# A shifted copy of v in an attention and gMLP kernel: engine copies or SBUF-to-SBUF transfers

## The chip, the core and the metric

The kernel runs on one core of a Trainium2 chip. The core has a matrix engine (TensorE, PE in the profile; its weight loads are PEld), a vector engine (VectorE, DVE), a scalar engine (ScalarE, ACT), a general engine (GpSimd, POOL) and a queue engine (SyncE, SP), which here issues nearly all DMA transfers. SBUF is the on-chip memory of 128 partitions, PSUM the accumulator memory of TensorE, used as 8 banks of 128 x 512 float32. Times are device microseconds of an execution; lower is better.

## The reference

Eight batches of eight heads, 576 positions and 64 features go through causal attention with a window of 64, then, with the heads side by side as 512 features, through a gMLP block (a gated layer that mixes positions with a 576 x 576 matrix).

```
scores = scale * q @ k.T                    # per batch and head, 576 x 576
mask   = (rel >= 0) & (rel < 64)            # rel = query position - key position
attn   = softmax(where(mask, scores, -1e9))
x      = attn @ v                           # heads laid side by side: 576 x 512
h      = relu(x @ w_in);  u, w = halves of h (512 columns each)
w_n    = (w - mean) / sqrt(var + 1e-6)      # over the 512 columns
w_s    = w_spatial @ w_n + b_spatial        # mixes the 576 positions
out    = (u * w_s) @ w_out
```

## The kernel before, in words

Every piece of work is a step with a name, a fixed piece of code and a set of engines that could do it (`Plan.add`, line 176). A text, `ORDER` (line 18), lists all 1117 steps in the order in which they are emitted. Each word is `name:engine:buffers`. `as_listed` (line 185) reads it and the loop at line 924 emits the steps. Every engine carries out its own steps strictly in that order, and semaphores hold a step until what it reads is there and the buffer that it writes is free. SP does the same with its list of transfers: an issue that has to wait holds up every later issue. `DQ` issues a transfer on SP as soon as its turn comes; `DG` does so behind the last matmul emitted ahead of it (`behind`, line 297), so the transfer is held back until TensorE has come that far.

The steps of a batch b, with the letters that the order uses, are these.

- ldq, ldk, ldv: loads of q and k (two halves of four heads each) and of v (five pieces of 128 positions, the last of 64). The v loads move runs of 64 float32, 256 bytes.
- cq, ck: casts of q and k to float16 (buffers nq, nk to hq, hk); tq, tk: transposes on VectorE into qT and kT.
- cv: the casts of v into `hv` (two steps of two pieces each). `hv` holds v in float16 as partition = position within 128, piece, head, feature.
- sl, su, s4: the copy of v shifted by 64 positions, `hs`. sl copies partitions 0 to 63 of pieces 1 to 3 of hv to the same place in hs, su copies partitions 64 to 127 of each piece of hv to the same partitions of the next piece of hs, and s4 casts the last 64 positions straight from the load. So piece c of hs holds positions 128c to 128c+63 in its lower half and the 64 positions ahead of them in its upper half; no row changes its partition.
- S: the scores of four heads in blocks of 64 keys, in four PSUM banks; E: the exponentials on ScalarE; M: the mask, a minimum on VectorE; Z: row sums by a matmul with ones; N and n: logarithm and exponential that turn a row sum into its inverse; P: attention times v; X: the product with the inverse, into x. A suffix r is the last 64 positions of all heads.
- P reads keys in blocks of 128 positions that start at multiples of 64. Even starts come from hv and odd starts from hs, which is why the shifted copy is needed: `vv = hv.t if c % 2 == 1 or c == 0 else hs.t` (line 592 on).
- V and U: the two halves of x @ w_in, Vr and Ur their ReLU on ScalarE; Vb and Va the mean and variance on VectorE (tiles st and mv); L1 and L2 the inverse root; A the normalization (tile vn); G: w_spatial times vn; Ge: the gate (tile g); O: times w_out; Oe: evacuation on ScalarE; st: the store.

Batch 0 gets hv in another way (`run_steps`, line 484): v is loaded in long runs (ldx), cast (cx), and put in order by matmuls with a selection matrix (pick, Y), and evacuated (F). Its shifted copies are engine copies too (sl0_0x, su0_0x and so on). Weights are loaded (ldwin, ldwsp, ldwo), cast (cwin, cwsp, cwo), and w_spatial is transposed on TensorE (W) and evacuated (We, tile wspT).

The work of the batches overlaps: while TensorE does V, U, G and O of one batch, the attention of the next is under way. A copy helper, `cp` (line 301), picks the engine's form of copy; on POOL it cuts a cast of q or k into three instructions and one of v into one for each piece. `cost` (line 314) lists the engines that a copy may go to. The buffers are few: two each of hv, hs and of the v load, eight of the other loads (`BUFS`, line 152).

The copies of v for batches 1 to 7 are made in `value_steps` (line 441). In the order before, they stand on these engines: batch 1 on POOL (sl1_0) and VectorE (three), batch 2 on POOL and ScalarE (sl2_1), batch 4 on POOL and ScalarE (sl4_0), batch 6 on POOL and ScalarE (sl6_1, su6_1), and batches 3, 5 and 7 on POOL alone.

Of the kernel before, what the change touches and what calls it, by code (L numbers as in the profile page):

```python
# [18 lines left out]
D0:PE:0 D1:PE:1 ldk0_0a:DQ:0 ldx0_0:DQ:0 D2:PE:2 ldk0_0b:DQ D3:PE:3 D4:PE:4 ldq0_0a:DQ:1 ldq0_0b:DQ  # L19
ldk0_1a:DQ:2 cq0_0a:POOL:0 D5:PE:5 pick:DVE:0 D6:PE:6 ck0_0a:ACT:1 D7:PE:7 D8:PE:0 tk0_0a:DVE:0  # L20
ldq0_1a:DQ:3 D9:PE:0 D10:PE:0 D11:PE:0 ck0_0b:ACT cx0_0:DVE:2 D12:PE:0 D13:PE:0 ldq0_1b:DQ D14:PE:0
ldk0_1b:DQ Y0_0:PE:0:1:2:3 cq0_0b:POOL F0_00:ACT:0 ldx0_1:DQ D15:PE:4 ck0_1a:POOL:3 tk0_0b:DVE
F0_01:ACT ldwsp0:DQ:4 D16:PE:4 D17:PE:4 ldwsp2:DQ:5 tq0_0a:DVE:1 F0_02:DVE D18:PE:4 tq0_0b:DVE
ldwsp1:DQ:6 ldwin10:DQ:7 ldv0_4:DQ D19:PE:4 F0_03:ACT D20:PE:4 cq0_1a:DVE:1 sl0_0x:ACT:0
tk0_1a:DVE:2 D21:PE:4 cq0_1b:POOL tq0_1a:DVE:3 D22:PE:4 cwsp0:POOL ck0_1b:DVE ldwin11:DQ:0
tq0_1b:DVE D23:PE:4 S0_0:PE:4:5:6:7 E0_02:ACT:0 tk0_1b:DVE E0_03:ACT E0_00:ACT:1 S0_1:PE:0:1:3:2
E0_01:ACT su0_0x:DVE M0_00:DVE cwin110:POOL ldq1_0:DG:1 cx0_1:ACT:2 E0_10:ACT:2 Y0_1:PE:6:7:4:5
ldk1_0:DG:3 M0_01:DVE E0_12:ACT:3 F0_12:DVE E0_11:ACT F0_10:DVE S0_r:PE:0:4:3:6 cwsp4:DVE D24:PE:1
ldb:DQ:2 E0_13:ACT E0_r0:ACT:0 M0_10:DVE cwin111:POOL Z0_01:PE:1 D25:PE:2 cwsp1:DVE M0_11:DVE
ldwin01:DQ:5 Z0_00:PE:2 E0_r1:ACT E0_r2:ACT cwsp3:DVE F0_11:ACT cq1_0:POOL:0 cwsp2:DVE E0_r3:ACT  # L30
Z0_10:PE:0 N0_01:ACT:0 N0_10:ACT:1 Z0_11:PE:4 F0_13:ACT ldwin00:DQ:4 N0_00:ACT:2 M0_r:DVE P0_01:PE:3
W4:PE:7 W3:PE:6 sl0_1x:DVE n0_01:ACT su0_1x:DVE n0_00:ACT P0_00:PE:1 N0_11:ACT:3 P0_11:PE:0
n0_10:ACT cwin010:POOL cwin101:DVE Z0_r:PE:5 P0_10:PE:2 We3:DVE n0_11:ACT s40_:DVE X0_00:DVE:1
P0_r:PE:6 W2:PE:4 N0_r:ACT:4 W1:PE:1 cwin100:ACT W0:PE:5 ldk1_1:DG:6 X0_01:DVE X0_10:DVE:2
ldq1_1:DQ:0 We4:DVE V0a_3:PE:3 We0:ACT X0_11:DVE V0a_2:PE:2 V0a_0:PE:7 ck1_0:ACT:1 We2:DVE
tq1_0:DVE:4 V0b_2:PE ldwo0:DQ:7 tk1_0:DVE:5 We1:ACT V0b_3:PE n0_r:ACT V0a_1:PE:5 V0b_0:PE ldwo1:DQ:1
ldv1_0:DG:1 Vr0_2:ACT:0 X0_r:DVE:0 Vr0_0:ACT:1 ldv1_1:DG cwin011:POOL V0b_1:PE S1_0:PE:0:4:1:2
ldv1_2:DQ Vr0_3:ACT:2 cwin000:POOL Vr0_1:ACT:3 ldv1_3:DG Vb0_2:DVE:0 V0_4:PE:6 E1_00:ACT:0
Vr0_4:ACT:4 Vb0_0:DVE:1 Vb0_3:DVE:2 cwin001:POOL Va0_2:DVE E1_02:ACT:1 E1_03:ACT Vb0_1:DVE:3
U0_4:PE:7 Va0_3:DVE E1_01:ACT ldv1_4:DG ck1_1:POOL:3 Vb0_4:DVE:4 Va0_0:DVE Va0_1:DVE Va0_4:DVE  # L40
cb:POOL tk1_1:DVE:0 U0_3:PE:3 L10:ACT:0 ldk2_0:DG:3 L20:ACT cq1_1:ACT:2 U0_0:PE:5 U0_1:PE:0
A0_2:DVE:0 cwo00:ACT U0_2:PE:6 ldq2_0:DQ:5 A0_0:DVE:1 A0_4:DVE Ur0_1:ACT:0 Ur0_0:ACT:1 Ur0_3:ACT:2
ldq2_1:DQ:4 A0_3:DVE:2 A0_1:DVE:3 tq1_1:DVE:1 Ur0_4:ACT:3 cwo01:POOL Ur0_2:ACT:4 G0_0:PE:1
S1_1:PE:2:4:0:5 M1_01:DVE E1_10:ACT:3 E1_11:ACT Ge0_0:DVE:0 E1_12:ACT:2 Z1_01:PE:3 G0_3:PE:7
S1_r:PE:6:1:2:4 E1_13:ACT M1_00:DVE cv1_0:DVE:1 M1_10:DVE G0_1:PE:0 cwo11:POOL E1_r0:ACT:1
sl1_0:POOL:1 Z1_10:PE:5 N1_01:ACT:5 Z1_00:PE:6 E1_r1:ACT G0_4:PE:3 ldk2_1:DQ:6 Ge0_3:DVE:1 G0_2:PE:7
N1_10:ACT:2 M1_11:DVE Z1_11:PE:1 N1_00:ACT:0 E1_r2:ACT su1_0:DVE ldq3_0:DG:2 n1_00:ACT s41_:ACT
ldk3_0:DG:0 cv1_1:DVE su1_1:DVE sl1_1:DVE cwo10:POOL ck2_0:POOL:0 P1_10:PE:5 n1_10:ACT E1_r3:ACT
ldv2_0:DQ:0 Ge0_4:DVE:2 Ge0_1:DVE:3 ldv2_1:DG N1_11:ACT:1 Ge0_2:DVE:4 P1_11:PE:6 n1_01:ACT
cq2_1:POOL:1 X1_10:DVE:3 cq2_0:ACT:3 P1_00:PE:2 ck2_1:POOL:2 P1_01:PE:3 O0_2:PE:0 ldv2_2:DQ  # L50
X1_00:DVE:0 Oe0_2:ACT:0 O0_0:PE:4 tk2_0:DVE:2 ldv2_3:DG O0_3:PE:7 tq2_0:DVE:3 O0_1:PE:1 Oe0_0:ACT:1
n1_11:ACT X1_01:DVE Oe0_3:ACT X1_11:DVE S2_0:PE:5:2:0:4 Oe0_1:ACT V1_3:PE:7 E2_00:ACT:3 V1_2:PE:3
V1_0:PE:1 tq2_1:DVE:0 E2_02:ACT:2 E2_01:ACT V1_1:PE:6 M2_00:DVE M1_r:DVE Vr1_3:ACT:5 E2_03:ACT
tk2_1:DVE:1 Vr1_0:ACT:6 Vb1_0:DVE:5 Vr1_2:ACT:7 P1_r:PE:5 cq3_0:POOL:0 Vr1_1:ACT:0 Z1_r:PE:0
S2_1:PE:2:7:4:1 ldv2_4:DQ U1_3:PE:3 N1_r:ACT:3 n1_r:ACT M2_01:DVE E2_12:ACT:0 Z2_00:PE:6 E2_13:ACT
Vb1_1:DVE:0 X1_r:DVE:1 E2_10:ACT:1 ck3_0:POOL:3 V1_4:PE:0 Ur1_3:ACT:5 Z2_01:PE:4 Vb1_3:DVE:1
Vr1_4:ACT:1 M2_11:DVE Vb1_2:DVE:2 Va1_3:DVE U1_4:PE:5 N2_01:ACT:4 U1_1:PE:1 Va1_1:DVE E2_11:ACT
Vb1_4:DVE:0 U1_2:PE:2 Va1_2:DVE ldq3_1:DG:7 Va1_0:DVE cv2_0:POOL:0 N2_00:ACT:2 Va1_4:DVE L11:ACT:1
M2_10:DVE sl2_0:POOL:0 Ur1_4:ACT:1 L21:ACT ldk3_1:DQ:1 S2_r:PE:3:4:7:6 Ur1_1:ACT:2 A1_0:DVE:4
# [904 lines left out]
```

## Time and profile before

| | |
|---|---|
| three runs | 201.89, 202.25, 204.39 us; median 202.25 us |
| profiled execution | 204.64 us, of which the span from first to last instruction is 202.9 us |
| mean granted TensorE clock | 0.975 |
| busy share of the span | PE 93%, VectorE 81%, ScalarE 80%, POOL 40% |
| DMA | 42.67 MB, 69.4% of the 16 engines' span in the SP queue |

Busy time is the time in which at least one instruction of an engine is under way. Matmuls overlap, so a matmul's own time is longer than the distance to the next one. The windows view gives busy time, granted clock, DMA share and bytes per second in any stretch; the tile view gives the shortest, median and longest instruction on one buffer; the waits view names who waited for whom; the timeline gives the instructions by start (the first number) and length (the second), with the idle time ahead of one in brackets. A DMA's landing time runs from its issue to its completion.

### The profile page before, as it was taken

The page shows a single profiled execution, that of the slowest core. Times are in us where ns is not written, and L with a number is a line of the kernel's source. Part 1 is how long each engine was busy: PE and PEld are TensorE (multiplying, and loading weights), DVE is VectorE, ACT ScalarE, POOL GpSimd, SP SyncE. Part 2 cuts the span into 40 slices and gives each one's busy share as a digit, 9 for nine tenths or more (in the row PEclk, how much of TensorE's full clock was granted, in tenths as well). Part 3 has the DMA queues.
Part 4 walks back from the last instruction along what each step waited for, and adds up shares of the span by engine and source line. Part 5 has one row for each costly group of instructions (what it writes and reads, how often), then busy time and mean ns, then how long its engine had stood idle before and what let it go on. Part 6 is the DMA issues. An engine that isn't in the chain of part 4 may idle for free.

```text
span 202.9 us, 7046 instructions
## 1 busy us (share of the span) xinstructions
PE 187.9 (93%) x2935; PEld 97.8 (48%) x2935; DVE 165.2 (81%) x322; ACT 163.0 (80%) x342; POOL 81.6 (40%) x146
## 2 busy tenths in 40 slices
PE   7839998989999999899999999999999999999991
PEld 2333744444446454444654456554554554544450
DVE  6598899999999997996999999979875995466421
ACT  3277999897999999979989999899999494873341
POOL 4221556268752529962555395611970100000000
PEclk9965799999999999999999999999999999999999
DMA  6999999999619999936697998599901500114344
GB/s 190 348 340 283 381 399 241 257 371 296 128 12 305 296 347 195 258 118 237 189 335 175 270 316 158 113 304 335 240 5 50 215 3 0 29 36 167 134 185 154
DMA packets 46977, 42.67 MB, mean 210 GB/s; under 512 B 34529, under 2 KB 35681, under 8 KB 46946
## 3 DMA queue, kind: packets, MB, share of 16 engines
q1 hardware_dynamic: 46722, 41.90, 69.4%
q8 instruction: 23, 0.38, 0.8%
q10 hardware_dynamic: 224, 0.33, 0.5%
q14 instruction: 8, 0.07, 0.1%
HBM read 32.79 MB, written 9.44 MB: 208 GB/s over the span
## 4 chain that ended last, share of the span: by engine, by line
PE 46%; DVE 29%; ACT 12%; DMA 7%; issue 3%; SPq 1%; POOL 0%; DVEq 0%; ACTq 0%; POOLq 0%
PE bank L295 45%; DVE x L605 5%; DVE qT L433 4%; DMA out_dram<-ob 4%; DVE vn L799 4%; ACT e L568 4%; DVE kT L433 3%; DVE st L728 3%; DVE g L859 3%; DMA nq<-in_q_dram 3%; DVE e L573 2%; ACT lz L612 2%; ACT vs L726 2%; DVE hv L312 1%; ACT lz L614 1%
## 5 line engine op out<-in xcount | busy, mean ns | idle before, releaser
L295 PE MATMUL bank<-wspT,vn 128*128 128x512 f16 (+3 forms) x320 | 43.4, 286 | 1.6 <-DVE vn L799 1.5
L295 PE MATMUL bank<-wout,g 128*128 128x512 f16 (+2 forms) x164 | 39.3, 375 | 0.4 <-DVE g L859 0.2
L295 PE MATMUL bank<-win,x 128*128 128x512 f16 (+1 forms) x160 | 38.4, 380 | 0.2 <-ACT e L568 0.2
L568 ACT ACTIVATE e<-bank 128x512 f16<-128x512 f32 x64 | 35.3, 611 | 3.4 <-PE bank L295 3.0
L859 DVE TENSOR_TENSOR g<-bank,ru 128x512 f16<-128x512 f32 (+1 forms) x40 | 24.2, 625 | 13.2 <-PE bank L295 7.3
L295 PE MATMUL bank<-x,win 128*128 128x64 f16 (+1 forms) x256 | 34.9, 286 | 0.0
L728 DVE BATCH_NORM_STATS2 st<-vs 128x6 f32<-128x512 f16 (+1 forms) x40 | 26.7, 676 | 8.7 <-ACT vs L726 8.3
L703 ACT COPY ob<-bank 128x512 f32<-128x512 f32 (+1 forms) x39 | 22.7, 589 | 10.6 <-PE bank L295 9.1
L295 PEld LDWEIGHTS <-vn 128*128 128x128 f16 (+1 forms) x320 | 20.1, 97 | 21.0 <-DVE vn L799 2.3
L310 POOL COPY hs<-hv 64x512 f16<-64x512 f16 x36 | 22.9, 660 | 11.9 <-ACT hv L303 7.0
L726 ACT ACTIVATE vs<-bank 128x512 f16<-128x512 f32 (+1 forms) x40 | 23.5, 608 | 4.7 <-PE bank L295 4.4
L573 DVE TENSOR_TENSOR e<-e,mask 128x1024 f16<-128x1024 f16 x32 | 22.7, 721 | 2.3 <-ACT e L568 2.3
L828 ACT ACTIVATE ru<-bank 128x512 f32<-128x512 f32 (+1 forms) x40 | 21.3, 561 | 3.5 <-PE bank L295 3.4
L295 PEld LDWEIGHTS <-win 128*128 128x128 f16 x256 | 15.9, 98 | 15.7 <-issue 2.1
L307 POOL CAST hk<-nk 128x384 f16<-128x384 f32 x30 | 16.3, 580 | 16.7 <-ACT ob L703 8.5
L295 PEld LDWEIGHTS <-x 128*128 128x128 f16 (+1 forms) x160 | 14.9, 100 | 16.5 <-issue 1.1
L433 DVE STREAM_TRANSPOSE kT<-hk 128x576 f32<-128x576 f32 (+1 forms) x18 | 20.1, 1117 | 2.6 <-ACT hk L303 2.2
L295 PEld LDWEIGHTS <-g 128*128 128x128 f16 (+1 forms) x164 | 14.9, 100 | 14.7 <-DVE g L859 1.3
L295 PE MATMUL bank<-qT,kT 32*64 32x128 f16 (+2 forms) x1280 | 16.6, 225 | 5.6 <-ACT e L568 2.3
L605 DVE TENSOR_TENSOR x<-bank,lz 128x512 f16<-128x512 f32 x32 | 20.6, 671 | 1.0 <-ACT lz L614 1.0
L295 PEld LDWEIGHTS <-kT 32*64 32x64 f16 x1280 | 13.6, 107 | 15.1 <-issue 8.8
L433 DVE STREAM_TRANSPOSE qT<-hq 128x576 f32<-128x576 f32 (+1 forms) x18 | 20.1, 1118 | 0.2
(83 smaller groups left out, 256.1 us busy)
## 6 DMA issues: line engine op xcount, KB each, us to landing
nq<-in_q_dram SPq DMA_DIRECT2D x14, 576.0 KB, 5.7
nk<-in_k_dram SPq DMA_DIRECT2D x14, 576.0 KB, 6.2
nv<-in_v_dram SPq DMA_DIRECT2D x28, 256.0 KB, 6.7
out_dram<-ob SPq DMA_DIRECT2D x14, 512.0 KB, 4.3
wi<-in_moe_w_in_dram SPq DMA_DIRECT2D x4, 512.0 KB, 10.3
nk<-in_k_dram SPq DMA_DIRECT2D x4, 288.0 KB, 6.8
nq<-in_q_dram SPq DMA_DIRECT2D x4, 288.0 KB, 6.8
ws<-in_moe_w_spatial_dram SPq DMA_DIRECT2D x2, 576.0 KB, 9.1
```

The lines of the kernel that those rows point to most:

```text
L295: last[0] = nc.tensor.matmul(*a, **kw)
L307: nc.gpsimd.tensor_copy(o[:, n:n + w], i[:, n:n + w])
L310: nc.gpsimd.tensor_copy(o[:, c, :, :], i[:, c, :, :])
L433: lambda e, cs=cs, j0=j0, j1=j1: nc.vector.transpose(qt.t[:, :].rearrange("p (i j) -> p j i", j=18)[:, j0:j1, :], h.t[:, cs].bitcast(f32). ...
L568: lambda e, u=u, w=w: nc.scalar.activation(e2[u].t[:, w, :], sc[2 * u + w].t[:, :], AF.Exp, bias=0.0, scale=0.125),
L573: mins.append(add(f"M{b}_{g}{u}", ("DVE", 0.65), key, lambda e, u=u: nc.vector.tensor_tensor(e2[u].t[:, :, :], e2[u].t[:, :, :], mask[:, : ...
L605: lambda e, u=u, ob=ob, lz=lz: nc.vector.tensor_tensor(x.t[:, u, :], ob.t[:, :], lz.t[:, :], ALU.mult),
L703: lambda e: (nc.vector.tensor_copy if last else nc.scalar.copy)(view(), m.t[rows, 0:n]),
L726: rl = add(f"Vr{b}_{j}", ("ACT", 0.49), key, lambda e: nc.scalar.activation(vs.t[0:jn, :], m.t[0:jn, :], AF.Relu), deps=[pv], acq=[vs], us ...
L728: s1 = add(f"Vb{b}_{j}", ("DVE", 0.6), key + 0.02, lambda e: nc.vector.bn_stats(st6.t[0:jn, 0:6], vs.t[0:jn, :]), deps=[rl], acq=[st6], us ...
L828: lambda e, m=m, ru=ru, n=n: nc.scalar.activation(ru.t[:, 0:n], m.t[:, 0:n], AF.Relu), deps=[pu], acq=[ru], uses=[m])))
L859: lambda e, m=m, g=g, ru=ru, n=n: nc.vector.tensor_tensor(g.t[:, 0:n], m.t[:, 0:n], ru.t[:, 0:n], ALU.mult),
```

## The change

For batches 1 to 7 the four engine steps sl and su go. Two transfers that SP issues take their place, from SBUF to SBUF: xl copies partitions 0 to 63 (3 KB each), xu partitions 64 to 127 (4 KB each, one piece on). Both wait for both casts of v. s4 stays an engine cast and is listed as dependent on xl.

```diff
         for n, (lo, hi) in enumerate([(0, 2), (2, 4)]):
             w = hi - lo
-            l0 = max(lo, 1)
-            c = add(f"cv{b}_{n}", cost(512 * w, d=early), key + 0.003,
...
-            sl = add(f"sl{b}_{n}", cost(512 * (hi - l0), d=early), key + 0.0035,
-                     lambda e, l0=l0, hi=hi: cp(e, hs.t[0:64, l0:hi, :, :], hv.t[0:64, l0:hi, :, :]),
-                     deps=[c] + done[1:2], acq=[] if done else [hs],
-                     uses=[hv] + ([hs] if done else []))
-            su = add(f"su{b}_{n}", cost(512 * w, d=early), key + 0.0035,
-                     lambda e, lo=lo, hi=hi: cp(
-                         e, hs.t[64:128, lo + 1:hi + 1, :, :], hv.t[64:128, lo:hi, :, :]),
-                     deps=[c, done[1] if done else sl], uses=[hv, hs])
-            done += [c, sl, su]
+            done.append(add(f"cv{b}_{n}", cost(512 * w, d=early), key + 0.003,
...
+        done.append(add(f"xl{b}_", ("DQ", 0.45), key + 0.0035, lambda e: nc.sync.dma_start(
+            hs.t[0:64, 1:4, :, :], hv.t[0:64, 1:4, :, :]), deps=done[:2], acq=[hs], uses=[hv],
+            nbytes=0.5, n=64))
+        done.append(add(f"xu{b}_", ("DQ", 0.45), key + 0.0036, lambda e: nc.sync.dma_start(
+            hs.t[64:128, 1:5, :, :], hv.t[64:128, 0:4, :, :]), deps=done[:3], uses=[hv, hs],
+            nbytes=0.65, n=64))
```

`ORDER` is written anew as a whole: 28 steps leave it, 14 enter, and 1103 remain. The steps of TensorE are the same 294, in another sequence. Of the others, 42 change their engine, most of them in the stage that loads the weights and the first two batches; among the loads, 36 change between DQ and DG. Around the transfers of batches 1 and 2 the new order reads so (TensorE's, SP's and the cast steps among others):

```
ldv1_1:DG ... ldv1_2:DG ... S1_0:PE ... ldv1_3:DQ ldq2_0:DQ ... ldk2_0:DQ ... ldv1_4:DQ ... ldwo1:DQ
... cv1_0:POOL ... ldwo0:DQ ... S1_r:PE ... S1_1:PE ... U0_1:PE ... cv1_1:DVE ... G0_3:PE ... G0_2:PE ...
Z1_00:PE Z1_11:PE ... xl1_:DQ Z1_10:PE ... G0_0:PE ... xu1_:DQ G0_4:PE ldk2_1:DG ... G0_1:PE ldq2_1:DG
s41_:POOL ... ldv2_0:DG S2_0:PE ... P1_10:PE ... P1_00:PE ldk3_0:DG ldv2_1:DG ... P1_11:PE ... P1_01:PE
... P1_r:PE ... O0_0:PE O0_1:PE ... O0_2:PE ... V1_0:PE V1_2:PE V1_3:PE
... cv2_1:POOL V1_1:PE S2_1:PE ... V1_4:PE ... xl2_:DQ ... S2_r:PE ... U1_1:PE ldv2_4:DG ... xu2_:DQ ...
U1_4:PE ... U1_0:PE ... O0_3:PE ... U1_2:PE ... U1_3:PE ... Z2_10:PE Z2_01:PE ... Z2_11:PE ... Z2_r:PE ... P2_01:PE
```

In the first loads, x of batch 0 (ldx0_0) now comes first, then three pieces of q, and then the pieces of k (ldk0_0b is the sixth transfer). Before, k and q alternated, and ldq0_0b was the fifth. The order of the loads of w_out against those of v of batch 1 is reversed: ldwo1 and ldwo0 now come behind ldv1_4. S2_0 now stands ahead of P1_10, and O0_3 behind U1_0; before, O0_3 came with the other O0 steps ahead of S2_0. For batch 5 the order is st2_4, ldv6_0 (DG), ldv5_4 (DG), xu5; for batch 7 it is ldv7_4 (DG), cv7_1 (POOL), xl7, xu7.

More of the change, by code (lines that the diff above doesn't have):

```diff
@@ L18 @@
 ORDER = """
[L19 to L59, printed above, removed]
@@ new lines @@
+Z1_11:PE:5 cwo11:POOL N1_00:ACT:2 N1_01:ACT:0 n1_00:ACT Ge0_3:DVE:0 xl1_:DQ:1 Z1_10:PE:7 Ge0_2:DVE:1
+cwo10:POOL G0_0:PE:3 tq2_0:DVE:2 xu1_:DQ G0_4:PE:6 ldk2_1:DG:4 N1_11:ACT:1 Ur0_1:ACT:4 N1_10:ACT:3
+G0_1:PE:0 ldq2_1:DG:5 s41_:POOL tk2_0:DVE:3 n1_11:ACT ldv2_0:DG:0 S2_0:PE:1:4:5:2 n1_10:ACT
+P1_10:PE:7 Ge0_0:DVE:2 Ge0_1:DVE:3 P1_00:PE:3 ldk3_0:DG:3 ldv2_1:DG cwo00:ACT E2_00:ACT:2 P1_11:PE:0
+Ge0_4:DVE:4 P1_01:PE:6 cwo01:POOL X1_10:DVE:3 ldv2_2:DG n1_r:ACT P1_r:PE:1 cq2_1:POOL:2 E2_02:ACT:0
+ldv2_3:DQ n1_01:ACT ck2_1:ACT:0 cv2_0:POOL:0 ck3_0:POOL:3 X1_r:DVE:1 ldq3_0:DQ:2 X1_11:DVE
```

214 lines of the change are left out of this document (123 added, 91 removed).

## The prediction

> **What bounds the kernel now.** I read the page first (spans and slices), then busy time by windows, then the DMA queue, then the tiles that the change touches. The profiled execution has a span of 202.9 us and a time of 204.64 us, so 1.74 us lie around the span. It stands 2.39 us above the median of the runs, 202.25 us; the sum is made against 204.64 and then carried over to the median.
>
> ```profile
> PE 187.9 (93%) x2935; PEld 97.8 (48%) x2935; DVE 165.2 (81%) x322; ACT 163.0 (80%) x342; POOL 81.6 (40%) x146
> 0.00:10.00 10.00, 8.00 (x40) 3.12 (x41) 6.08 (x27) 3.44 (x6) 3.66 (x13) 1.00 0.81 267
> 10.00:20.00 10.00, 6.37 (x186) 3.56 (x187) 9.48 (x21) 7.64 (x16) 2.00 (x3) 0.61 1.08 314
> 20.00:30.00 10.00, 9.69 (x187) 5.98 (x182) 8.98 (x16) 9.42 (x19) 5.11 (x9) 0.88 1.03 386
> 30.00:40.00 10.00, 9.13 (x147) 4.36 (x146) 10.00 (x22) 9.08 (x20) 4.23 (x7) 1.00 1.00 248
> 40.00:50.00 10.00, 9.11 (x180) 4.80 (x178) 9.89 (x16) 8.50 (x18) 7.54 (x14) 1.00 1.03 349
> 8.50:55.90 47.40, 40.57 (x793) 21.57 (x791) 45.41 (x82) 41.03 (x86) 25.06 (x42) 0.89 0.98 302
> 66.00:123.00 57.00, 55.00 (x897) 29.00 (x892) 53.20 (x91) 53.09 (x114) 34.73 (x59) 1.00 0.89 249
> 151.30:193.30 42.00, 42.00 (x423) 20.76 (x423) 26.05 (x59) 26.86 (x59) 0.61 (x1) 1.00 0.22 76
> ```
>
> The columns after the length are the busy times of PE, PEld, DVE, ACT and POOL, the granted clock, the DMA share and GB/s. Three regimes are to be seen. From 8.5 to 55.9 us VectorE is full (45.41 of 47.40) and so are the DMA engines (share 1.00 and more from 10 to 50 us). From 66 to 123 us TensorE leads (55.00 of 57), with VectorE and ScalarE close behind. From 151.3 to 193.3 us TensorE has no gap at all. POOL, which does nearly all of the shifted copies, bounds nothing: 40%.
>
> **What the copies cost today.**
>
> ```profile
> L310 POOL COPY hs<-hv 64x512 f16<-64x512 f16 x36 | 22.9, 660 | 11.9 <-ACT hv L303 7.0 <-DVE hv L312 4.0
> L303 ACT COPY hs<-hv 64x1024 f16<-64x1024 f16 x3 | 3.1, 1042 | 0.0
> L303 ACT COPY hs<-hv 64x512 f16<-64x512 f16 x1 | 0.6, 616 | 0.0
> L312 DVE COPY hs<-hv 64x1024 f16<-64x1024 f16 x5 | 2.8, 561 | 0.1
> PEld L295 <- DVE hs L312: 1.1, 2, 0.8
> PE bank L295 <- DVE hs L312: 0.9, 2, 0.7
> 43.94 0.22 PE L295 MATMUL bank<-e,hs 128*64 128x64 f16 x2 [0.65 <-DVE hs L312]
> ```
>
> All 36 POOL copies go (22.9 us), all four ACT copies (3.7 us), and three of the five large DVE copies (batch 1's; 3 x 0.561 = 1.7 us). TensorE waited for hs in two places only, 0.9 us in all, the longer at batch 1 (43.94). So the 22.9 us taken off POOL are worth **0 on the path**: POOL stands idle 60% of the span, and TensorE's other work covers them. The cover was thin at batch 1 alone.
>
> **Casts that change engine.** 42 steps do. On VectorE, besides the three copies, there leave: the tail copy of batch 0, the first cast of v for batch 1, one hx cast, one cast each of hq and hk, two wnat casts, two hv evacuations, a win cast, three wspT evacuations, and the building of pick (ten small operations, which ran ahead of the loads). Three hv, one wnat, one hx and two wspT come in.
>
> ```profile
> L312 DVE CAST hv<-nv 128x1024 f16<-128x1024 f32 x2 | 1.7, 841 | 0.0
> L312 DVE CAST hv<-bank 128x256 f16<-128x256 f32 x3 | 1.2, 416 | 0.4 <-PE bank L295 0.4
> L312 DVE CAST wnat<-ws 128x576 f16<-128x576 f32 x3 | 1.3, 445 | 0.0
> L312 DVE CAST hs<-nv 64x512 f16<-64x512 f32 x1 | 0.8, 826 | 0.0
> L312 DVE COPY wspT<-bank 128x576 f16<-128x576 f16 x2 | 0.9, 448 | 0.0
> ```
>
> Out: 1.7 copies + 0.84 + 0.83 + wspT 3 x 0.45 + wnat 2 x 0.45, and estimated from these rows 0.68 for hx, 0.9 for hq and hk, 0.4 for win, and 2 x 0.42 for hv = 8.4 us. In: 3 x 0.42 + 0.45 + 0.68 + 2 x 0.45 = 3.3 us. Net VectorE loses some 5.1 us, nearly all of it before 56 us, where it was full. ACT loses the 3.7 us of copies; I count the casts that it gives (17 steps) and gets (18) as equal, since they are of like sizes.
>
> **Why the 5.1 us do not come back whole: the landing of the transfers.** In the new order 12.7 MB stand in SP's queue ahead of xl1: batch 0 and w_spatial 4.9, w_in 2.1, q, k and v of batch 1 3.5, half of q and k of batch 2 1.2, w_out 1.05; xl1 and xu1 add 0.46. By the five windows above 2.67 + 3.14 + 3.86 + 2.48 = 12.15 MB had moved by 40 us, then 349 GB/s: 13.2 MB are through at 40 + 1.05/0.349 = 43.0 us. The last packet is then reported with a lag that I bound by landings in a queue nearly empty:
>
> ```profile
> out_dram<-ob SPq DMA_DIRECT2D x3, 256.0 KB, 2.2
> nv<-in_v_dram SPq DMA_DIRECT2D x28, 256.0 KB, 6.7
> DMA to landing us min/median/max: 2.8/6.3/10.6
> L454 SPq DMA_DIRECT2D nv<-in_v_dram x35: 368/830/5397, 28.3 to 154.8; - x35
> 44.13 6.55 SPq L454 DMA_DIRECT2D nv<-in_v_dram  x4
> 105.73 0.87 PE L295 MATMUL bank<-qT,kT 32*64 32x128 f16 x64
> 44.95 3.71 PE L295 MATMUL bank<-wout,g 128*128 128x512 f16 x16
> 49.60 3.19 PE L295 MATMUL bank<-win,x 128*128 128x512 f16 x14
> ```
>
> So xu1 lands at 44 to 45 us, I take 44.5; the matmuls of P1 that need hs started at 43.94 before. TensorE has 0.87 us more behind it there (S2_0 now stands ahead of P1), so P1 is worth **about 0** (-0.3), whatever VectorE has saved. After P1 the saving shows: the P steps with the remainder (about 1.1 us; 43.94 to 44.95 before, without the remainder), then three O0 steps of 3.71/4 = 0.93, bring V1 to 44.5 + 3.9 = 48.4 us, against 49.60 before; 0.93 (O0_3) is postponed against 0.87 done earlier. VectorE's backlog, which ran on to 55.9 us, is gone. I take **-1.0**, bounds -5.1 (all of VectorE's) and +1.
>
> **The transfers of batches 2 to 7.** Fourteen issues, 64 partitions of 3 KB (192 KB) and of 4 KB (256 KB), together 3.2 MB, 7.5% of the 42.67 MB. Issues cost SP some 0.4 us each; SP idles long elsewhere, so 0. What counts is the time from the issue of xu to the first P that needs it. xl waits for both casts, and xu stands behind it; where a held load ("DG") stands just ahead of xu, it is issued only when TensorE has come that far. TensorE's work between, at 0.87 to 0.93 us for four matmuls of 512 columns and 1.1 for G: batch 2 4.8 us (behind ldv2_4), batch 3 14, batch 4 about 10, batch 5 5.3 (behind ldv5_4), batch 6 7.9, batch 7 about 5.5 (behind the cast cv7_1). The issue of the v load ahead takes 0.83 us in the median, xu's own 0.4, the landing 2.2 in an empty queue and 6.3 (median of nv) in a full one: 3.4 to 7.5 us. Batches 3, 4 and 6 are covered. At 2 and 5 I take 5.3 us, nearer to the low end since few loads stand ahead there: **+0.5 each**, bounds 0 and +2.7 each. Batch 7: 0, since the DMA share past 151 us is 0.22. If the cover of batch 3, 4 or 6 went, each would cost what 7.5 us exceed it by.
>
> The Trainium skill (page "DMA: Bandwidth & Descriptors", section "Rules for kernel authors") says that two transfers to disjoint partition halves serialize over the same engines and are better made as one, which speaks against xl and xu; its fit of 2.0 us plus bytes over 436 GB/s gives 2.6 us for xu, an estimate. By that the two +0.5 would vanish and the sum end 1 us lower; the 6.7 us of the nv row show that in this queue it does not hold under load.
>
> **Queue order on SP.** Behind xl1, which waits for the casts of v (v1's fourth part lands only near 37 us), now stand ldk2_1, ldq2_1 and the v loads of batch 2; S2_1 is the first to need them, some 9 us of TensorE's work after P1. Hidden: 0. Without that cover each us of delay would go into S2_1. The head: x of batch 0 is loaded first and the k parts come after three q parts, so the last piece S0_0 needs is the sixth, not the fifth: 0.29 MB later, +0.9 us at 314 GB/s; VectorE has three casts fewer ahead of the first mask, -1. Taken as **0**, bounds -1 and +1.
>
> **66 to 151 us.** VectorE and ScalarE are at 93% there, and POOL's copies seem to stretch VectorE:
>
> ```profile
> L799 DVE TENSOR_SCALAR vn<-vs,mv,ln x40: 342/400/1764, 33.4 to 185.8; 128x512 f16<-128x512 f16 x32, 64x512 f16<-64x512 f16 x8
> L573 DVE TENSOR_TENSOR e<-e,mask x32: 653/678/1089, 14.4 to 162.4; 128x1024 f16<-128x1024 f16 x32
> L799 DVE TENSOR_SCALAR vn<-vs,mv,ln 128x512 f16<-128x512 f16 x32 | 14.7, 499 | 1.6 <-ACT ln L789 1.6
> L573 DVE TENSOR_TENSOR e<-e,mask 128x1024 f16<-128x1024 f16 x32 | 22.7, 721 | 2.3 <-ACT e L568 2.3
> ```
>
> Means above medians: 32 x 0.10 + 32 x 0.04 = 4.5 us of VectorE in the whole span; with 28% of POOL's busy time gone, 1.3 us less. With ACT's 3.7 us I take **-1.0** of TensorE's 2 us of gaps in 57, bounds 0 and -3. The Trainium skill ("SBUF — State Buffer", section "Who interferes with whom") calls this an exclusive lock between GpSimd and VectorE's copies, casts and two-input operations; the maxima of 1764 and 1089 ns agree, and by that rule alone the gain would be the same 1.3 us. The last 50 us are TensorE's alone: 0.
>
> **Sum**: -1.0 - 1.0 + 1.0 + 0 = -1.0 us: 203.6 against the profiled 204.64, **201.2** against the median.
>
> **Rivals.** (1) *Faster.* The landing does not bind P1, and VectorE's 5.1 us come back in the stretch where it was 96% busy, with nothing lost at batches 2 and 5: some 4.8 us, 197.5 us. For it: the windows before 56 us. Against it: the bytes ahead of xl1, which decides once less than 12 MB stand there. (2) *Slower.* The transfers land like the loads in the same queue, 7.5 us after their anchor: P2 waits 7.5 - 4.8 = 2.7, P5 2.2, and P1 1.7 more because its landing lags like the nv row; 6.6 us less the 2.0 gained gives +4.6, 206.8 us. It decides once the landing at two of these places is over 6 us. For it: the median of 6.3 us, and SP's issues of v loads that stood for up to 5.4 us (44.13: four issues took 6.55). Against it: the empty-queue row of 2.2. (3) *Hidden anyway*: no transfer is waited for and nothing is gained, since TensorE's gaps have other causes: 202.2.
>
> **How the numbers follow.** The forecast (two gains of 1 us, half of them given back) with rival 3 beside it, both within 2%: 0.45. Slower: 0.33. Faster: 0.22. The bound of 2% (4 us) is about what a measurement of this kernel can tell from no change. The likeliest case alone runs from 199 to 204; the range reaches to both rivals, 197.4 to 207.0.
>
> **What would show it.** Right: VectorE's busy time down by some 5 to 6 us and POOL's by 10 or more; P1's hs matmuls at 44 to 45 us waiting for a DMA; V1 about 1 us earlier; waits of TensorE for DMA hs<-hv under 1 us at batches 2 and 5; 42 us without a gap at the end. Wrong: waits for hs<-hv of over 2 us at several batches (rival 2), P1 before 42 us (rival 1), or casts on POOL that are late because loads queued behind xl are.

## The result and the profile after

The changed kernel takes 209.69 us (median of four executions, 209.09 to 210.29) beside 202.65 us of the kernel before in the same session: a ratio of 1.034, interval 1.026 to 1.041. Executions of one kernel scatter by some per cent with different granted clocks, so each time below is the median of all of them and each ratio compares the quicker ones alone. The changed kernel is slower by 7.0 us, where 1 us of gain was forecast, and lies outside the forecast's range. The profiled execution after has 209.09 us and a span of 207.2; that of before, 204.64 us, lay 2 us above its median, so these two differ by 4.4 us only, and that much is what their traces can show.

The page after, busy times and the load queue:

```profile
PE 188.8 (91%) x2935; PEld 98.8 (48%) x2935; DVE 158.0 (76%) x305; ACT 158.6 (77%) x339; POOL 64.0 (31%) x127
q1 hardware_dynamic: 47842, 45.12, 75.2%
```

Every engine that was to be relieved is relieved: VectorE by 7.2 us, ScalarE by 4.4, POOL by 17.6. Now by windows, first the kernel before in two stretches that were not shown, then the one after (columns as in the prediction):

```profile
0.00:41.00 41.00, 34.19 (x561) 17.20 (x562) 35.51 (x85) 30.17 (x62) 16.00 (x33) 0.88 0.98 306
41.00:57.00 16.00, 14.71 (x281) 7.72 (x279) 15.72 (x23) 14.52 (x29) 12.43 (x23) 1.00 0.81 241
```

```profile
0.00:41.00 41.00, 33.74 (x561) 16.64 (x561) 32.71 (x72) 29.95 (x65) 20.04 (x47) 0.88 0.95 296
40.00:50.00 10.00, 5.86 (x153) 3.77 (x155) 6.03 (x9) 6.21 (x14) 3.75 (x7) 0.95 1.04 267
41.00:57.00 16.00, 12.23 (x194) 6.87 (x193) 11.22 (x16) 10.65 (x21) 7.58 (x14) 0.89 1.05 259
66.00:123.00 57.00, 55.15 (x989) 29.40 (x984) 52.14 (x91) 50.39 (x110) 23.74 (x42) 1.00 0.92 257
157.00:199.00 42.00, 41.79 (x388) 20.64 (x374) 24.30 (x55) 25.08 (x54) 0.00 (x0) 1.00 0.24 84
```

At 41 us both kernels have issued 561 matmuls. Then, in 16 us, TensorE is busy 12.23 us instead of 14.71 and has the lower clock, 0.89. From 66 to 123 us nothing is won or lost (55.15 and 55.00 of 57), and the end is nearly without a gap as before. So the place is 41 to 57 us. What stood there, in the timeline of the kernel after (start, length, idle time before in brackets):

```profile
38.57 0.52 SPq L464 DMA_DIRECT2D hs<-hv  x1
39.15 1.08 SPq L467 DMA_DIRECT2D hs<-hv  x1
48.80 0.22 PE L292 MATMUL bank<-e,hs 128*64 128x64 f16 x2 [3.57 <-DMA hs<-hv]
...
83.59 0.61 POOL L307 CAST hv<-nv 128x512 f16<-128x512 f32 x1 [6.78 <-DMA nv<-in_v_dram]
84.23 0.48 SPq L464 DMA_DIRECT2D hs<-hv  x1
85.93 0.62 SPq L467 DMA_DIRECT2D hs<-hv  x1
89.94 0.22 PE L292 MATMUL bank<-e,hs 128*64 128x64 f16 x2 [1.55 <-DMA hs<-hv]
```

The transfers of batch 1 were issued at 38.6 and 39.1 us, and TensorE stood for them until 48.80. A second, shorter wait comes at batch 3, because a piece of v landed late and POOL's cast, and so the issue, with it. These two are all of the waits for hs (total, times, longest); the second row is the time from issue to landing of the transfers, of which the longest, 9.5 us, is that of batch 1's xu, landed at 48.66 us:

```profile
PE bank L292 <- DMA hs<-hv: 5.1, 2, 3.6
DMA to landing us min/median/max: 2.7/4.8/9.5
```

The long wait costs more than its length, which the granted clock shows (the third column from the end):

```profile
45.00:48.70 3.70, 0.23 (x12) 0.12 (x4) 0.68 (x2) 0.62 (x1) 1.50 (x3) 1.00 1.00 268
48.70:52.00 3.30, 3.20 (x72) 2.34 (x73) 1.84 (x4) 2.71 (x5) 0.49 (x2) 0.54 0.89 239
52.00:54.00 2.00, 2.00 (x10) 0.87 (x9) 2.00 (x3) 0.73 (x2) 1.47 (x4) 0.91 1.11 320
```

After the gap the clock is 0.54 for 3.3 us and 0.91 for 2.0: 3.3 x 0.46 + 2.0 x 0.09 = 1.7 us of TensorE's work more. The Trainium skill ("TensorE: Matmul & The Clock Gate", "Part 1: The HAM clock gate") says that after an idle window of some 3.4 us the array runs at half clock until it has been busy about as long; these rows agree. Other traces of this case show that the window needn't be idle (last section).

### The profile page after: what moved, and what is told of

Its sections match the earlier page's. It is cut to its first block, busy times and chain, and to the rows that moved or that the text cites. A ratio compares the mean times of both kernels' runs of the same rounds, so it can differ in the third digit from the quotient of the medians.

```text
span 207.2 us, 7010 instructions
## 1 busy us (share of the span) xinstructions
PE 188.8 (91%) x2935; PEld 98.8 (48%) x2935; DVE 158.0 (76%) x305; ACT 158.6 (77%) x339; POOL 64.0 (31%) x127
## 4 chain that ended last, share of the span: by engine, by line
PE 52%; DMA 19%; ACT 15%; issue 5%; DVE 3%; SPq 2%; POOL 2%; POOLq 0%; ACTq 0%; DVEq 0%
PE bank L292 51%; DMA nq<-in_q_dram 5%; ACT e L561 5%; DMA hs<-hv 5%; DMA ws<-in_moe_w_spatial_dram 4%; DMA nk<-in_k_dram 3%; ACT vs L719 2%; DMA nv<-in_v_dram 2%; ACT ru L821 2%; ACT ob L696 2%; POOL hq L304 1%; PE bank L381 1%; ACT lz L607 1%; ACT lz L605 1%; SPq L451 1%
## 5 line engine op out<-in xcount | busy, mean ns | idle before, releaser
L292 PE MATMUL bank<-wspT,vn 128*128 128x512 f16 (+3 forms) x320 | 42.6, 286 | 0.2
L561 ACT ACTIVATE e<-bank 128x512 f16<-128x512 f32 x64 | 36.1, 605 | 8.1 <-PE bank L292 8.1
L292 PE MATMUL bank<-win,x 128*128 128x512 f16 (+1 forms) x160 | 39.1, 380 | 0.2 <-ACT ru L821 0.2
L292 PE MATMUL bank<-x,win 128*128 128x64 f16 (+1 forms) x256 | 35.9, 286 | 0.2 <-ACT e L561 0.2
L566 DVE TENSOR_TENSOR e<-e,mask 128x1024 f16<-128x1024 f16 x32 | 21.8, 699 | 3.4 <-ACT e L561 3.4
L821 ACT ACTIVATE ru<-bank 128x512 f32<-128x512 f32 (+1 forms) x40 | 22.3, 572 | 1.3 <-DVE g L852 1.2
L304 POOL CAST hq<-nq 128x384 f16<-128x384 f32 x33 | 15.9, 522 | 17.7 <-DMA nq<-in_q_dram 17.6
L307 POOL CAST hv<-nv 128x512 f16<-128x512 f32 x22 | 13.8, 633 | 24.3 <-DMA nv<-in_v_dram 24.0
```

The source lines that it names most:

```text
L292: last[0] = nc.tensor.matmul(*a, **kw)
L304: nc.gpsimd.tensor_copy(o[:, n:n + w], i[:, n:n + w])
L307: nc.gpsimd.tensor_copy(o[:, c, :, :], i[:, c, :, :])
L561: lambda e, u=u, w=w: nc.scalar.activation(e2[u].t[:, w, :], sc[2 * u + w].t[:, :], AF.Exp, bias=0.0, scale=0.125),
L566: mins.append(add(f"M{b}_{g}{u}", ("DVE", 0.65), key, lambda e, u=u: nc.vector.tensor_tensor(e2[u].t[:, :, :], e2[u].t[:, :, :], mask[:, : ...
L821: lambda e, m=m, ru=ru, n=n: nc.scalar.activation(ru.t[:, 0:n], m.t[:, 0:n], AF.Relu), deps=[pu], acq=[ru], uses=[m])))
```

## The experiments

Five theories were at stake. 1: the loss is the waits for transfers that land late. 2: it is the new order and the moved casts, whoever copies. 3: the transfers' load slows the other loads. 4, formed after the first runs: several arrivals for 41 to 57 us are late together, and taking one wait away uncovers the next. 5: TensorE waits for its own instructions, fetched behind the loads.

Times are medians; the ratio is to the kernel before in the same session, with its interval. Where no interval is given, the extremes of the executions stand in brackets.

**Does the wait for hs make the loss, or the new order?** Three kernels: the new order with engine copies, the old order with transfers, and the changed kernel with nobody reading what is transferred.

```diff
# copies_in_new_order: ORDER of after, steps of before
-xl1_:DQ:1 ... xu1_:DQ            (all seven batches)
+cv1_0:... sl1_0:POOL:1 su1_0:POOL ... cv1_1:... sl1_1:POOL su1_1:POOL
```

> The changed kernel's order and cast engines, but each pair of transfers replaced by engine copies on POOL right behind the cast of v that they read. Theory 1 (the transfers' late landing is what costs, 5.1 us of TensorE waits at P1 and P3): 203 to 205.5 us, no wait for hs above 1 us. Theory 2 (the new order and the moved casts cost the time, whoever makes the copy): 208 us or more. Theory 3 (the 3.2 MB more on the DMA engines slow the loads): 203 to 205.5 us too, since the transfers are gone.

Measured: 208.76 us, ratio 1.027 (1.018 to 1.035). Theory 1, that the transfers' waits are the loss, falls in this form: without any transfer the same order loses 5 to 6 us. In the execution that was traced the loss lies in the same place (window and stalls of this kernel); that one took 211.28 us, the other three 207.02, 207.68 and 209.83, and whether they stood there as long isn't recorded:

```profile
41.00:57.00 16.00, 11.71 (x200) 6.23 (x196) 11.98 (x17) 11.14 (x22) 10.00 (x18) 1.00 0.85 230
```

```profile
45.83 0.77 PE L290 MATMUL bank<-qT,kT 32*64 32x128 f16 x64 [1.29 <-DVE kT L428]
52.80 1.02 PE L290 MATMUL bank<-wout,g 128*128 128x512 f16 x4 [3.00 <-issue]
```

The first stall is the copies' own doing (POOL casts k of batch 2 only behind four copy instructions, from 39.03 to 43.01 us); the second has no releaser among the engines and is taken up below.

```diff
# xfer_in_old_order: ORDER of before
-sl1_0:POOL:1 ... su1_0:DVE ... su1_1:DVE sl1_1:DVE   (and so for batches 2 to 7)
 cv1_1:DVE
+xl1_:DQ:1 xu1_:DQ
```

> The order and cast engines of before, with the copies of batches 1 to 7 replaced by the two transfers behind the second cast of v (the tail cast s4 of batches 1, 2 and 4 moved behind them). Theory 1: slower than before by more than 4 us, 207 to 213 us, because batch 1's P comes right behind the cast and waits out a landing of 5 to 9 us. Theory 2: 201 to 203.5 us. Theory 3: 204 to 206 us, spread over the span instead of sitting at P.

Measured: 232.41 us, ratio 1.145 (1.139 to 1.151), 30 us more than before, where the theories allowed 10 at most. Three waits make it, at batches 1, 2 and 4:

```profile
53.52 0.27 PE L288 MATMUL bank<-e,hs 128*64 128x64 f16 x2 [11.54 <-DMA hs<-hv]
82.62 0.27 PE L288 MATMUL bank<-e,hs 128*64 128x64 f16 x2 [5.94 <-DMA hs<-hv]
126.63 0.26 PE L288 MATMUL bank<-e,hs 128*64 128x64 f16 x2 [9.93 <-DMA hs<-hv]
```

So the new order is a good part of the price of the transfers: it makes room for them, and without it they are far worse.

```diff
# after_no_reader (part of the attention is computed from the unshifted v)
-vv = hv.t if c % 2 == 1 or c == 0 else hs.t
+vv = hv.t
-HS[b, g].t[:, 4, 4 * g + 2 * u + w, :]
+HV[b, g].t[:, 3, 4 * g + 2 * u + w, :]
```

> The changed kernel with every transfer still made, but P reads hv where it would read hs (also in the remainder), so that nothing waits for a transfer; part of the attention output is computed from unshifted v. Theory 1: the 5.1 us of waits go, 203.5 to 206 us. Theory 2: 209 to 210 us. Theory 3: 208 to 210 us, since the bytes still move.

Measured: 210.72 us (207.21 to 211.11; before 202.86). Taking the wait away gave nothing back in three of the four executions (210.68 us and more); the fourth took 207.21. In the one of the three that was traced, the next late arrivals stand behind it; on TensorE and on ScalarE:

```profile
48.84 0.32 PE L288 MATMUL bank<-er,hv 128*64 128x64 f16 x8 [1.76 <-ACT e L557]
52.05 1.02 PE L288 MATMUL bank<-wout,g 128*128 128x512 f16 x4 [1.06 <-issue]
```

```profile
47.67 0.62 ACT L296 CAST wout<-wo 128x512 f16<-128x512 f32 x1 [1.52 <-DMA wo<-in_moe_w_out_dram]
51.97 1.15 ACT L296 CAST hk<-nk 128x1152 f16<-128x1152 f32 x1 [1.86 <-DMA nk<-in_k_dram]
```

ScalarE stands in order behind casts whose loads (w_out, then k of batch 2) land at 47.7 and 52 us, and the exponentials behind them hold TensorE. Theory 4 was formed here.

**Another queue.** xfer_by_pool issues the transfers from POOL, xfer_by_act from ScalarE:

```diff
-add(f"xl{b}_", ("DQ", 0.45), key + 0.0035, lambda e: nc.sync.dma_start(
+add(f"xl{b}_", ("POOL", 0.45), key + 0.0035, lambda e: nc.gpsimd.dma_start(   # or ACT, nc.scalar
```

> The changed kernel with the transfers issued by POOL instead of SP, at the same places. They no longer stand behind the loads in SP's queue, nor do loads stand behind them. Theory 1: landing 2 to 3.5 us instead of 4.8 in the median, TensorE's waits for hs under 2 us in all, 203.5 to 206.5 us. Theory 2: 209 to 210 us. Theory 3: 208 to 210 us.

> The changed kernel with the transfers issued from ScalarE's list, at the same places of the order, so that they stand in another queue than the loads. In the changed kernel xl1 and xu1 were issued at 38.6 and 39.1 and landed at 48.7, behind 1.05 MB of w_out in the same queue; with w_out behind them they landed 3.4 us after their issue. If the queue's order makes the difference, they land at 43 to 45 us here too, and the time is 205-208. If it is the load on the engines whatever the queue (theory 3), they land at 47 us or later, 209-211. Each issue costs ScalarE some of its time and may make it wait for the casts, which could cost another 1 to 5 us (POOL's issue cost 10).

Measured: 219.85 us, ratio 1.080 (1.070 to 1.089), and 222.31 us, ratio 1.095 (1.088 to 1.103). In order on a computing engine the issues come late: on POOL at 44.43 and 45.64, behind casts that wait for loads, and TensorE waits 8.43 us until 54.09 for hs; on ScalarE at 43.6, and later it stands itself for POOL's cast of v:

```profile
82.64 0.47 ACTq L460 DMA_DIRECT2D hs<-hv  x1
83.15 0.60 ACT L715 ACTIVATE vs<-bank 128x512 f16<-128x512 f32 x1 [6.80 <-POOL hv L303]
```

xfer_by_act came out worse than I expected. A queue of their own didn't bring the transfers in sooner either: on POOL's the first pair landed 6.6 and 8.3 us after its issues, and over all batches the times to landing were

```profile
DMA to landing us min/median/max: 2.9/7.1/8.9
```

On ScalarE's queue xu1 landed 5.8 us after its issue. In both kernels the loads of SP's queue were under way beside them (DMA share 0.95 and 0.97 ahead of 50 us). So it isn't the place in one queue alone that makes a landing late, but also what is being loaded at that time.

**The place behind w_out.**

```diff
# wo_behind_xu1: ORDER of after
-ldv1_4:DQ ... ldwo1:DQ:1 ... ldwo0:DQ:6 ... cwo11:POOL ... xl1_:DQ:1 ... cwo10:POOL ... xu1_:DQ ... s41_:POOL
+ldv1_4:DQ ... xl1_:DQ:1 ... xu1_:DQ ldwo1:DQ:1 ldwo0:DQ:6 ... s41_:POOL cwo11:POOL cwo10:POOL
```

> The changed kernel with the two loads of w_out behind xu1 instead of ahead of xl1, and two of the casts of w_out behind the tail copy of batch 1. Theory 1 (the wait for hs is the loss): xu1 lands some 3 to 4 us earlier, P1 does not wait, and the time falls to 205-207. Theory 4 (removing one wait lets the next stand): w_out lands 2 us later, O0 and ScalarE behind cwo00 wait for it, and the time stays at 208.5-211. Theory 3 (3.2 MB more slow all loads): no change, 209-210.

Measured: 206.26 us, ratio 1.011 (1.006 to 1.016). This edit gives back 2.3% of the 3.4%. With the loads, two casts of w_out move behind the tail copy s41 on POOL; in the changed kernel that copy was done at 45.9 us, 2.8 us ahead of the landing, so its place held up nothing there. Issues and stalls of this kernel, and its window, from an execution of 208.26 us:

```profile
39.03 0.53 SPq L460 DMA_DIRECT2D hs<-hv  x1
39.61 0.81 SPq L463 DMA_DIRECT2D hs<-hv  x1
40.47 1.34 SPq L391 DMA_DIRECT2D wo<-in_moe_w_out_dram  x2
```

```profile
47.64 0.32 PE L288 MATMUL bank<-er,hs 128*64 128x64 f16 x8 [1.27 <-ACT e L557]
...
65.19 0.22 PE L288 MATMUL bank<-e,hs 128*64 128x64 f16 x2 [2.39 <-DMA hs<-hv]
```

```profile
41.00:57.00 16.00, 14.28 (x307) 7.85 (x304) 13.38 (x22) 13.98 (x27) 8.37 (x16) 1.00 0.99 279
```

xu1 landed at 43.0, 3.3 us after its issue, and not 9.5; w_out, now issued at 40.5 instead of 34.7, landed at 46.5, as in the changed kernel (46.6), so it lost nothing. Instead of 3.57 us TensorE stands 1.27, and the clock stays at 1.00. The next wait, at 65 us, is again a transfer, behind a held load of v; behind it the clock is 0.50 from 66.3 to 69.7 us.

```diff
# xu_behind_xl: wo_behind_xu1, and for batches 2 to 7
-xl2_:DQ:0 ldv2_4:DG xu2_:DQ
+xl2_:DQ:0 xu2_:DQ ldv2_4:DG
# all_mended: besides, ldk2_1 and ldq2_1 not held, behind ldwo0, and ck2_1 on POOL, not on ScalarE
```

> wo_behind_xu1 (206.26 us) with xu of every batch from 2 on directly behind its xl in SP's list, no longer behind the held tail load of v. In wo_behind_xu1 TensorE stood 2.57 us at 65.19 us for the hs of batch 2, whose xu was issued only behind ldv2_4. Theory 1 (what is lost is lost at the landings): the stall at 65 us goes or shrinks below 1 us, 203.5-205.5. Theory 4 (removing one wait lets the next stand): another wait takes its place, 206-207.

> The same, and the second halves of k and q of batch 2 stand right behind the w_out loads without a hold, and the cast of that half of k is POOL's. Theories 1 and 4 together say that the changed kernel's loss is a few late arrivals at 41 to 66 us; then this one comes within 1.5 us of the kernel before, 202.5-204.5. If the transfers cost something wherever they stand (theory 3), 205-207.

Measured: 207.16 us, ratio 1.011 (1.003 to 1.018), and 206.62 us, ratio 1.016 (1.008 to 1.024). The stall at 65 us is gone in the trace of the first; in its place there is one of 2.1 us at 48.3, for exponentials, with the clock at 0.50 for 3.4 us behind it. In the trace of all_mended (an execution of 209.00 us) a wait of 2.0 us for hs stands at 65.8 again. For xu_behind_xl theory 4 holds again. all_mended should have come within 1.5 us of the kernel before by theories 1 and 4; it lies 3 us above it, where theory 3 had put it. None of the three comes below the kernel before.

**Which part of the new order?** w_out's loads to the old place ahead of v1, then k and q of batch 2 early as well, with copies and with transfers; and the converse in the old order.

```diff
# copies_w_out_first: copies_in_new_order with
+ldwo0:DQ:7 ldwo1:DQ:0 ldv1_0:DQ:1 ... ldq2_0:DQ:1 ldk2_0:DQ:6 ldv1_4:DQ
# copies_w_out_k2_first, after_w_out_k2_first: besides
+ldv1_4:DQ ldk2_1:DQ:4 ldq2_1:DQ:5 ... ck2_1:POOL:0 cq2_1:POOL:2
# copies_k2_first: only the second
# before_w_out_late: before, with after's ldq2_0 ldk2_0 ldv1_4 ldwo1 ldwo0, casts of w_out behind
```

> The copies_in_new_order kernel (the new order, engine copies) with one edit in the order of the loads: the two loads of w_out stand ahead of the v loads of batch 1, as in the kernel before, and the halves of q and k of batch 2 take their places; casts stay where they were. Theory 4 (of the 5 to 6 us that the new order loses whoever copies, nearly all arise between 41 and 57 us, because w_out, k and q of batch 2 and the casts that wait for them in order on ScalarE come late there): w_out then lands near 35 us instead of 43.7 to 45.0, cwo00 no longer holds up ScalarE, and the time falls from 208.8 to 205-206.5; what is left comes from the second half of k of batch 2. Theory 2 in its old form (the casts' engines and the other moves cost, spread over the kernel): 208-209.5, no change. Theory 5 (TensorE stands for its own instructions, which are fetched behind the loads: it resumed at 52.80 us 1.4 us after a fetch of 16 KB that had begun only at 50.2): the stall of 3 us stays as long as the DMA engines are full at 45 to 50 us, 207-209.

> The same, and the second halves of k and q of batch 2 stand without a hold right behind the v loads of batch 1 (36 us instead of 43.5), and the cast of that half of k is done by POOL, not by ScalarE ahead of two exponentials. Theory 4: the rest of the loss at 41 to 57 us goes too, 202.5-204.5, the same as before within 1%. Theory 2 in its old form: 208-209.5. Theory 5: since no load is then in the queue from about 48 us on, the fetch of instructions comes in time, 203-205; the two theories part only in the trace, by whether a gap of TensorE ends 1 to 1.5 us after a late fetch.

> The changed kernel itself (two transfers per batch) with the same edits of loads and cast. Theory 4 with Theory 1: w_out and the halves of k and q no longer come late, but the casts of v of batch 1 end some 2.6 us later (1.05 MB stand ahead of them), so xu1 is issued near 42 and lands at 48 to 50 us, and the first steps P wait for it as long as before (3 to 5 us): 207-210. If the transfers were free, it would come out like its twin with copies, within 1 us. Theory 2 in its old form: 209-211.

> copies_in_new_order (208.8 us) with the second halves of k and q of batch 2 behind w_out without a hold, and the cast of that half of k on POOL; w_out stays behind v of batch 1. Theory 5 (TensorE stood 3 us at 52.8 us for its own instructions, whose fetch began late because loads kept the DMA engines full): the loads now end before 48 us, the fetch begins by 48.5 and the stall of 3 us is gone, 205-207, as in copies_w_out_k2_first. If that stall has another cause, it stays at the same instruction of TensorE, 208-209.

> The kernel before with one thing of the new order: first halves of q and k of batch 2, the tail of v of batch 1 and then w_out, in the order of the changed kernel, in place of w_out ahead of v of batch 1; the four casts of w_out move behind accordingly (three on POOL, one on ScalarE ahead of O0). Theory 4 (late w_out and what waits for it in order cost 2 to 4 us): 205-207.5. If the late w_out is hidden in this order: 202.5-204.5, and the loss of the new order lies in the casts and the held loads.

Measured, in this order: 209.70 us, ratio 1.028 (1.020 to 1.036); 206.96, 1.015 (1.008 to 1.022); 208.72, 1.028 (1.019 to 1.037); 208.06 (206.12 to 210.18); 203.73, 1.002 (0.998 to 1.005). Theory 4 named w_out as the main part, and that was wrong twice: moved to the front it gives nothing with copies, and made late in the old order it costs nothing. With k and q early as well the time falls by some 2.5 us. Whether w_out has a part in that is open: with k and q alone two of the four executions took 206.12 and 206.48 us, no more than with both, and the other two 209.64 and 210.18. With the transfers less is gained; v, and so xu1, then comes later. What the remaining order and the moved casts cost isn't separated by these runs.

**What do the transfers cost that nobody waits for?**

```diff
# unread_in_before: the kernel before, its copies kept; behind cv{b}_1, from batch 1 on
+add(f"yl{b}_", ("DQ", 0.45), ..., nc.sync.dma_start(wsp_all[0:64, 0:1536], w_in_all[0:64, 0:1536]))
+add(f"yu{b}_", ("DQ", 0.45), ..., nc.sync.dma_start(wsp_all[64:128, 0:2048], w_in_all[64:128, 0:2048]))
# unread_twice_in_before: two such pairs; unread_four_in_before: four transfers of 64 x 2880 bytes
# short_waits_in_before: one transfer of 64 x 16 bytes out of hv, which waits for both casts of v
```

> The kernel before, unchanged in its copies and order, plus fourteen SBUF-to-SBUF transfers of the same rows (64 of 3 KB and 64 of 4 KB per batch, out of w_in into the natural w_spatial, which nobody reads any more) in SP's list behind the second cast of v of each batch from 1 on. They wait for nothing and nobody waits for them. Theory 3 (the transfers slow the loads: beside them packets of 4608 bytes took 300 to 360 ns instead of 183, and one pair kept the engines busy for some 3 us in which 1 MB of loads would have moved): 204.5-208, most of it at batches 1 and 2, where the DMA engines are full. Theory 1: 202-204, no more than the seven pairs' issue on SP.

> unread_in_before with two pairs per batch in place of one: 6.4 MB more instead of 3.2. Theory 3: the price doubles or more, 3 to 6 us over the kernel before, 206.5-209.5. If the 2 us came from something else (the place of four tiles, SP's issue), 204-206.

> unread_in_before with four transfers per batch of 64 rows of 2880 bytes, to places that don't overlap, so that SP waits for none: 5.2 MB more over the kernel in place of 3.2. Theory 3 with a price by bytes: 2.0 us x 5.2/3.2 = 3.3 us, 205.5-207.5. If it jumps as unread_twice_in_before did (26 us), the price is one of the engines' load after all: over 212.

> The kernel before with its copies, and in SP's list, behind the second cast of v of each batch from 1 on, one transfer of 64 rows of 16 bytes out of hv into a place that nobody reads. It moves nothing to speak of, but SP's list waits for the cast there, as it does for xl. The same list with the real transfers (xfer_in_old_order) took 29 us more than before, and waited 12.7 us for casts. If SP's waiting costs by itself (the loads behind it come late): 206-215. If only the landing of hs costs: 202.5-204.

Measured: 204.87 us, ratio 1.010 (1.002 to 1.018); 228.86 (224.17 to 230.24); 209.10, 1.029 (1.022 to 1.036); 203.02, 0.999 (0.995 to 1.003). By the ratios the load alone costs 2.0 us for 3.2 MB (0.5 to 3.6) and 5.9 for 5.2 MB (4.4 to 7.3). By the middle values that is more than in proportion, but the intervals allow proportion too, and twice as many transfers were issued. In the traces it is paid where TensorE leads and the DMA engines are 89% busy; the first row is unread_in_before, the second, in a fence of its own, unread_four_in_before:

```profile
66.00:123.00 57.00, 52.60 (x847) 27.59 (x847) 51.99 (x86) 50.43 (x107) 32.50 (x55) 1.00 0.95 258
```

```profile
66.00:123.00 57.00, 50.70 (x818) 26.17 (x816) 47.38 (x81) 47.94 (x105) 29.54 (x50) 0.97 0.95 268
```

Before, TensorE was busy 55.00 us here; 2.4 and 4.3 us are gone. SP's waiting for casts, on the other hand, costs nothing by itself: short_waits_in_before stood for them like this and took the same time as before.

```profile
SPq L475 <- POOL hv L307: 5.4, 2, 5.0
SPq L475 <- ACT er L643: 1.9, 1, 1.9
```

unread_twice_in_before tests something else than it was meant to: its second pair overlaps the first in its destination, and SP's list stood for the first to land, with all loads behind it:

```profile
SPq L481 <- DMA wnat<-win: 31.7, 7, 7.2
```

It took 26 us more than before, with twice the load. So some 7 us of waiting in SP's list fit in; 32, with that load, don't.

**Is it free late?**

```diff
# xfer_from_5_in_old_order: the kernel before; for batches 5 to 7 alone
-sl5_0 su5_0 sl5_1 su5_1
+xl5_:DQ xu5_:DQ                  (behind cv5_1)
```

> The kernel before with the two transfers in place of the copies for batches 5, 6 and 7 alone; batches 1 to 4 keep their copies, and the order is that of before. With transfers at all batches in this order TensorE stood 11.7, 6.1 and 10.1 us at batches 1, 2 and 4 and 0.7 at most later. Theory 1: no wait, 202.5-204.5. Theory 3: at most 0.9 us (three sevenths of 2), and the DMA engines are half idle there. A gain of over 1 us (below 202.5) would show that POOL's copies cost something there; I do not expect it, since TensorE has no gap behind 151 us.

Measured: 209.43 us, ratio 1.032 (1.026 to 1.039), against every theory. One wait makes it; SP's list and TensorE:

```profile
113.87 4.20 SPq L716 DMA_DIRECT2D out_dram<-ob  x1
118.17 1.85 SPq L448 DMA_DIRECT2D nv<-in_v_dram  x2
120.18 2.21 SPq L475 DMA_DIRECT2D hs<-hv  x1
122.44 0.59 SPq L478 DMA_DIRECT2D hs<-hv  x1
```

```profile
126.54 0.26 PE L289 MATMUL bank<-e,hs 128*64 128x64 f16 x2 [5.29 <-DMA hs<-hv]
```

The casts were done at 114.3 us, but a store and two loads stand ahead of xl5 in SP's list, and it came to its issue at 120.18. The DMA engines weren't half idle there, as I had expected: their share is 0.88 from 113.8 to 118 us and 1.01 until 120.2.

## Why the prediction was wrong, step by step

- *Landing bounds P1 at 44.5 us.* This is the step that failed: xu1 landed at 48.66. Two terms of it were mis-sized. The rate past 40 us was taken from the kernel before (349 GB/s) and came out at 267: by 41 us 41 x 0.296 = 12.1 MB had moved, and the 1.1 MB that were missing of 13.2 take 1.1/0.267 = 4.1 us, which gives 45.1 and not 43.0. The other 3.6 us stand against the 1 to 2 that I had added from landings in a nearly empty queue. I had let the queue pass in order, and it didn't: the trace's records show the first packet of the transfers at 42.4 and the last at 47.7, among the last ones of w_out and then beside the loads of k and q that stand behind them, of which 0.5 MB moved between 45.1 and 47.7 us. The report came 0.9 us later still. wo_behind_xu1 shows that the place matters: the same two transfers, with w_out behind them, landed 3.0 and 3.3 us after their issues.
- *V1 1 us earlier.* V1 started at 54.09 instead of 49.60. VectorE did lose 7.2 us (5.1 forecast), but at 41 us both kernels stand equally far; the DMA engines were nearly full in that stage before and after (share 0.98 and 0.95), which is the likely reason why a freer VectorE bought nothing there.
- *Order of the loads on SP: hidden, 0.* Wrong as a whole, right for SP's waiting alone (short_waits_in_before). The new order without transfers costs 5 to 6 us. I had priced each moved step by the instruction it delays, and not that ScalarE and POOL, in order, stand behind casts of late loads.
- *Transfers 2 to 7: 0.5 us each at batches 2 and 5, batches 3, 4 and 6 covered.* Batches 2 and 5 had no wait, and batch 3, with the longest lead (14 us), waited 1.55. The lead was counted from the casts' place in the order; v landed so late that the cast ran only at 83.59 us. For batch 5 the term didn't follow from its own figures: a landing of 5.3 us against a cover of 5.3 leaves nothing.
- *POOL's copies are worth 0, and 1 us is won from 66 to 123 us.* The first is right: 17.6 us less of POOL, no gap of TensorE gone. In the second VectorE does get quicker, by more than forecast:

```profile
L792 DVE TENSOR_SCALAR vn<-vs,mv,ln 128x512 f16<-128x512 f16 x32 | 12.2, 422 | 2.2 <-ACT ln L782 2.2
L566 DVE TENSOR_TENSOR e<-e,mask 128x1024 f16<-128x1024 f16 x32 | 21.8, 699 | 3.4 <-ACT e L561 3.4
```

  Means fell from 499 to 422 and from 721 to 699 ns, 3.2 us of VectorE against 1.3 forecast; with POOL's copies in the new order they were 526 and 748 (copies_k2_first). The window shows no gain for TensorE, because batch 3's wait of 1.55 us takes it back: without it 56.7 of 57 us would be busy, and wo_behind_xu1 and xu_behind_xl reach 56.6 and 56.5. But it isn't the copies' leaving that wins this: the new order with POOL's copies has the same,

```profile
66.00:123.00 57.00, 56.58 (x942) 29.48 (x940) 54.28 (x90) 50.31 (x110) 34.78 (x62) 1.00 0.80 224
```

  in copies_k2_first. For the transfers' load, which in the old order costs 2.4 us in that window (unread_in_before), the prediction had no term.
- *Tail: 0.* Right: TensorE is busy 41.79 of 42 us.
- *Rival 2 (slower, 206.8)* had the right sign and cause, transfers that land like loads; it put the waits at batches 2 and 5 and 1.7 us at batch 1, where they were 3.6 at batch 1 and 1.6 at batch 3, and it lacked the clock (1.7 us) and the load.

The account by ratios: 3.4% in all; 2.3% go when w_out stands behind the first transfers; 1.1% are left. These are as large as the 1.0% that the load alone costs in the old order, but that the two are the same isn't shown, and the window of 66 to 123 us speaks against it: there the load cost TensorE 2.4 us in the old order, and in the new one TensorE is as busy with the transfers as with copies. What is left may as well be the new order's own price (1.5% in copies_w_out_k2_first), or the one stall with a slow clock behind it that each trace of the three mended kernels still shows. Open is also why the new order with copies is nearly as slow as with transfers: in the one trace of it, one stall is its own copies on POOL, the other is told below, and the casts' part wasn't tried alone.
